# A second layer whose fourth product is also split once more: small sums of A22 by seeds and adding DMAs, a new order of 81 steps

## The chip, the cores and the metric

The kernel runs on one core of a Trainium2 chip. Its engines run side by side, each with its own queue of instructions that it takes strictly in order: TensorE (PE, matmuls; PEld is its weight loads), VectorE (DVE), ScalarE (ACT), GpSimd (POOL) and SyncE (SP, which issues most DMAs). They wait for one another on semaphores. Sixteen DMA engines move data for all queues. The metric is device time in microseconds (us).

## The reference, cut to what matters

```python
w = softmax(weight, axis=-1)                          # 8 heads x 7 taps
x_unf = x_pad[:, idx, :].reshape(B, S, K, H, group)   # B 8, S 4096, D 192
x = np.einsum('hk,bskhg->bshg', w, x_unf).reshape(B * S, D)
h = x @ w_in                                          # 32768 x 192 @ 192 x 2048
g = h * np.clip(h + 3.0, 0.0, 6.0) / 6.0
return (g @ w_out).astype(np.float32)                 # @ 2048 x 192
```

A causal convolution of seven taps along the tokens, one weight per head and tap, then a two-layer network with a hard swish between the layers. Everything is in 32-bit floats.

## The kernel before, in words

Tokens go in 32 blocks of 1024, two groups of 512. Block 0 is special (weights are rounded and loaded beside it, its second layer is direct); blocks 1 to 31 run the same loop: first layer, second layer.

**First layer** (`first_layer`, L443). Sixteen units of 18 matmuls; w_in and the convolved tokens y are split into high and low parts so that three fast passes make a product. A unit fills two banks of PSUM (one of four slots), ACT makes the clipped term from it (`relu`, L306), DVE multiplies (`gate`, L310), and g is in SBUF. Units 0 to 7 make A11 and A22 (token half and half of the 2048 hidden features), units 8 to 15 make A21 and A12; each Aij has eight chunks of 128 features by 512 tokens. Units 0 to 7 read `y_own`, units 8 to 15 read `y_other`, the same data with the upper and lower 64 partitions exchanged by DMA (`swap_parts`). Behind the units stand jobs: taps of the next block's convolution (L806, DVE, behind units 1, 5 and 9), the small sums of A11 (`small_sums`, L491, POOL), the differences S3 = A11 - A21 by pairs of chunks (`g_sums`, L380, POOL, the last pair on DVE), and S1 = A21 + A22 written over A21, for the first two pairs by a DMA from POOL that adds to what is there (L470), for the others by DVE (L400).

**Second layer** (`second_layer`, L502). Strassen's scheme with seven products P1 to P7 in place of eight: for example P4 = A22 x T4, P7 = S3 x T3, P2 = A12 x B21, P5 = S1 x T1. Each has 96 output columns, three strips of 32. PE is used as four strips (rows 0 to 31, 32 to 63 and so on of a PSUM bank) that work side by side. Strips 0 to 2 take plain products, one strip of columns each; strip 3 takes P1 and P5. Their first two strips of columns are done by Strassen *once more* (`level_two`, L591): even and odd chunks, the two strips of columns and the two halves of 512 tokens make a 2 by 2 scheme of seven small products, each four matmuls of 256 columns, on four small sums of the token side (128x1024 each) and four of the weights (`w_s`). Their third strip of columns is plain, eight chunks (for P1 five on strip 3 and one each on strips 0 to 2, bank e). Partial results are carried by ACT copies from a bank's rows to others (L608 to L614), where the next product adds on.

The order is written out by hand. `put(j, cost, fn)` gives a matmul to strip j and moves that strip's clock: cost 2 for 512 columns, 1 for 256. `do(t, fn)` places a job of another engine at time t of the same clock. All are sorted by clock and issued in that order (L686), so t says where an instruction stands in its engine's queue, and nothing waits for a clock: an engine starts the next instruction of its queue as soon as its semaphores allow. A second layer is 82 steps for each strip:

```python
        for q in range(NQ):
            plain(q, d, 4, q, every, True)
            before = (1, 6, NP)[q]
            plain(q, c, 7, q, every[:before], True)
            plain(q, e, 1, 2, range(5 + q, 6 + q))
...
            plain(q, a, 2, q, every[:6], True)
            plain(q, b, 6, q, every)
            plain(q, a, 2, q, every[6:])
```

Strip q does P4 (16 steps), P7 (16, reads S3), one chunk of P1's third strip of columns (2), P2 (12 and 4), P6 (16, reads S2 = S1 - A11) and P3 (16, reads a second S3 = A12 - S2). Banks are d, e, b, x_, a, c, two each from the PSUM slots of units 12, 13 and 14. The jobs: the split of the next y into high (ACT, L415) at 13 and low (DVE, L418) at 15, swaps to `y_other` (SP) at 18, the load of the x after next and its convolution's first taps from 20 on (L87, L804, L806), the four small sums of S1, written into A22 (`s5`), at 16.2, 30.5 and 34.5 (DVE), S2 and S3 (DVE) at 38, the results' adds, transposes and stores from 62.

Of the kernel before, what the change touches and what calls it, by code (L numbers as in the profile page):

```python
# [8 lines left out]
ALU = mybir.AluOpType  # L9
# [22 lines left out]
def kernel(  # L32
# [35 lines left out]
    xs = ctx.enter_context(tc.tile_pool(name="xs", bufs=1))  # L68
    ys = ctx.enter_context(tc.tile_pool(name="ys", bufs=1))
    ot = ctx.enter_context(tc.tile_pool(name="ot", bufs=1))  # L70
    ps = ctx.enter_context(tc.tile_pool(name="ps", bufs=1, space=bass.MemoryType.PSUM))
# [48 lines left out]
    w_in_parts = [cst.tile([P, NP, K3, P], F32, name=f"w_in{n}") for n in range(3)]  # L120
    y_own = [cst.tile([P, K3, N], F32, name=f"y{n}") for n in range(2)]
    y_other = cst.tile([P, 2, K3, N], F32, name="y_other")
    w_out = cst.tile([P, NP, 7, DH], F32, name="w_out")
    B11, B12, B21, B22, T1, T2, T4 = range(7)
    T3 = B12
    w_s = cst.tile([P, 2, 4, NP // 2, QS], F32, name="w_s")

    w_in_bits = moe_w_in.bitcast(U32).rearrange("(p s) (c f w) -> c p s f w", s=K3, f=P, w=2)
# [259 lines left out]
    def rows(q):  # L388
        return slice(q * QS, (q + 1) * QS)
# [51 lines left out]


    def first_layer(i, jobs):  # L443

        def unit(n):
            slot = free_slots.pop(0)
            for m_ in range(3):
                for s in range(K3):
                    products(n, slot, s, (m_,), s == 0, s == K3 - 1)
            to, both = places(n, slot)  # L450
            relu(to, both)
            gate(to, both)
            free_slots.append(slot)

        count = 2 * NP
        for job in jobs.get(-1, ()):
            job()
        for n in range(count):
            unit(n)
            for job in jobs.get(n, ()):  # L460
                job()
            if n == 1:
                s1.append(ot.tile([P, NP, N], F32, name="s1", tag="shared")[:])
            if n < NP and n % 2:
                small_sums(s1[-1], A11, (1, 2, 3, 4), nc.gpsimd, every[n - 1 : n + 1])
            if n > NP and n % 2:
                pair = slice(n - NP - 1, n - NP + 1)
                g_sums(nc.gpsimd if n + 1 < count else nc.vector, (3,), range(NP)[pair], 2)
                if n + 3 < count:
                    nc.gpsimd.dma_start(out=S1[:, pair], in_=A22[:, pair], accum_op=ALU.add)  # L470
        for pair in (slice(NP - 2, NP), slice(NP - 4, NP - 2)):
            add(S1[:, pair], A21[:, pair], A22[:, pair])

    TH = N // 2
# [17 lines left out]

    def small_weights(to, w):

        b11, b12, b21, b22 = (
            w_out[:, c::2, w, q * QS : (q + 1) * QS] for c in range(2) for q in range(2)
        )
        t1, t2, t3, t4 = (to[:, n] for n in range(4))
        for o, p, q in ((t1, b12, b11), (t2, b22, t1), (t3, b22, b12), (t4, b21, t2)):
            nc.gpsimd.tensor_tensor(out=o, in0=p, in1=q, op=ALU.subtract)  # L500

    def second_layer(i, between):  # L502
        last = i + 1 == NB
        ours = [free_slots.pop(0) for _ in range(3)]
        d, e, b, x_, a, c = (psum[:, 2 * n + k] for n in ours for k in range(2))
        ends = [psum[:, 2 * free_slots[0] + k] for k in range(2)] if last else [b, b]
# [34 lines left out]

        def small(n, m_, out, start=False):

            x, w = prod[n]
            sums, ws = (s1[-1], w_s[:, 0]) if n == 1 else (s5, w_s[:, 1])
            x11, x12, x21, x22 = four_parts(x)
            z1, z2, z3, z4 = four_parts(sums)
            b11, b12, b21, b22 = (
                w_out[:, h::2, w, q * QS : (q + 1) * QS] for h in range(2) for q in range(2)
            )  # L550
            t1, t2, t3, t4 = (ws[:, k] for k in range(4))
            xm, wm = {
# [3 lines left out]
            for u in range(NP // 2):  # L556
                put(3, 1, lambda u=u: matmul(
                    3, out[:, lo], wm[:, u], xm[:, u], start and u == 0
                ))
# [9 lines left out]
        def tiles():  # L569
# [3 lines left out]
            late.update(zip(("p7", "p5", "u3"), (results[0][m, n] for n in range(3))))  # L573

        for q in range(NQ):
            plain(q, d, 4, q, every, True)
            before = (1, 6, NP)[q]
            plain(q, c, 7, q, every[:before], True)
            plain(q, e, 1, 2, range(5 + q, 6 + q))
            do(clock[q], copy, out=e[rows(q + 1)] if q < 2 else p1[third], in_=e[rows(q)])  # L580
            plain(q, c, 7, q, every[before:])
            plain(q, a, 2, q, every[:6], True)
            plain(q, b, 6, q, every)
            plain(q, a, 2, q, every[6:])
            if last:
                plain_by_halves(q, 3, q, 0)
                plain_by_halves(q, 3, q, 1)
            else:
                plain(q, b, 3, q, every)

        def level_two(n, p, chunks, order):  # L591
# [25 lines left out]
            for step in order.split():  # L617
                if step[0] == "x":
                    fill(int(step[1]))
                elif step[0] in "lh":  # L620
                    fill_half("lh".index(step[0]), int(step[1]))
# [4 lines left out]

        level_two(1, lambda: p1, range(5), "1 x5 6 5 2 7 3 4")
        do(14, copy, out=e[first], in_=V)
        level_two(
# [4 lines left out]
        for t, job in between:  # L634
            do(t, job)
        for t, n in ((16.2, 1), (16.2, 2), (30.5, 3), (34.5, 4)):
            do(t, small_sums, s5, S1, (n,), nc.vector)
        do(32, tiles)
        do(34, lambda: copy(out=late["p7"], in_=c[m]))
        do(38, copy, out=b[m], in_=p1[:])  # L640
        do(38, g_sums, nc.vector, (2,), every, 4)
        do(38, g_sums, nc.vector, (4,), every, 4)
        do(62, lambda: add(late["u3"], b[m], late["p7"]))
        do(62, lambda: add(late["p7"], late["u3"], d[m]))
        do(62, lambda: store(i, late["p7"], 1, 0))
        do(66, add, p1[:], a[m], p1[:])
        do(66, lambda: store(i, p1, 0, 0))

# [33 lines left out]
        if last:  # L682
            do(74, end_lower)
        else:
            do(82, lambda: copy(out=late["p5"][third], in_=V))
        events = sorted(((t, fn) for st in streams for t, fn in st), key=lambda x: x[0])  # L686
# [28 lines left out]
    with tc.manual_schedule():  # L715
# [142 lines left out]

        def split_high():
            high_of(y_own[HIGH][:], y[:])  # L860

# [11 lines left out]
        def begin_block_two():  # L873
            w_sums(((T1, B12, B11), (T2, B22, T1), (T4, B21, T2)))
            for n, w in enumerate((B11, T1)):
                small_weights(w_s[:, n], w)
            conv.extend(conv_jobs(2))
            for job in conv[:3]:
# [16 lines left out]
        S3 = last.tile([P, NP, N], F32, name="s3")[:]  # L895
        p1 = last.tile([DH, N], F32, name="p1")
        left = []
        for i in range(1, NB):
# [10 lines left out]
            if i + 1 < NB:  # L909
                between = [(13, split_high), (15, split_rest), (18, swap_parts)]  # L910
            if i + 2 < NB:
# [35 lines left out]
```

## Time and profile before

| what | value |
|---|---|
| median of 3 runs | 2220.81 us (2220.73 to 2221.07) |
| profiled execution: time, span from first to last instruction | 2220.6 us, 2218.5 us |
| granted TensorE clock | 1.000 |
| PE, DVE, ACT, POOL busy | 2211.4, 1808.9, 935.8, 827.9 us |
| DMAs from SP and others, share of 16 engines (queue q1) | 105.86 MB, 23.7% |
| DMAs from POOL (queue q0) | 33.64 MB, 8.8% |
| one adding DMA (L470), 512 KB, issue to landing | 5.0 us median |

The chain of waits is the view to start with: it goes back from the last instruction to whatever released each one, and its shares say which engine set the end (PE 99%). A timeline lists one engine's instructions in order with their start and length, and in brackets the idle time ahead of one and who ended it. Windows give busy time per engine in stretches of time, then the granted clock, the share of the DMA engines, and GB/s. Matmuls in 32-bit floats appear as two passes each.

### The profile page before, as it was taken

The numbers are of one execution on the slowest core, as the hardware profiler recorded it, in microseconds if no ns is written. First come the engines' busy times: TensorE is split into PE (matmuls) and PEld (weight loads), VectorE is DVE, ScalarE is ACT, GpSimd is POOL, SyncE is SP. The second block draws the span as 40 slices with busy tenths as digits, with TensorE's granted clock in tenths as the row PEclk, the third lists the DMA queues.
The fourth block names the chain that finished last, engine by engine and source line by source line (L and its number), as shares of the span: only waits on it lengthen the run. The fifth ranks groups of instructions, "written<-read, shape, count | busy, mean of one in ns | idle before, by whom it ended". The sixth has DMA issues, their size and how long they took to land.

```text
span 2218.5 us, 49343 instructions
## 1 busy us (share of the span) xinstructions
PE 2211.4 (100%) x21598; PEld 1535.2 (69%) x21598; DVE 1808.9 (82%) x1588; ACT 935.8 (42%) x1172; POOL 827.9 (37%) x706
## 2 busy tenths in 40 slices
PE   9999999999999999999999999999999999999999
PEld 5567776677776677766777667776667776677766
DVE  8878788888888888888888888888888888888866
ACT  7434443344433444433444334443344433344433
POOL 4434442244422344323444224442244432344322
PEclk9999999999999999999999999999999999999999
DMA  7333323433223332243332333322433224333232
GB/s 165 65 71 69 66 37 67 77 63 77 35 58 78 70 70 49 44 77 70 70 62 40 68 74 66 77 35 59 77 68 73 43 49 77 70 70 57 40 59 34
DMA packets 249095, 142.91 MB, mean 64 GB/s; under 512 B 207120, under 2 KB 212240, under 8 KB 248880
## 3 DMA queue, kind: packets, MB, share of 16 engines
q1 hardware_dynamic: 230392, 105.86, 23.7%
q0 software_dynamic: 17248, 33.64, 8.8%
q8 instruction: 169, 2.77, 0.5%
q10 hardware_dynamic: 1240, 0.27, 0.1%
q14 instruction: 46, 0.38, 0.1%
HBM read 31.72 MB, written 25.17 MB: 26 GB/s over the span
## 4 chain that ended last, share of the span: by engine, by line
PE 99%; ACT 0%; DVE 0%; POOL 0%; DMA 0%; issue 0%; POOLq 0%; ACTq 0%; DVEq 0%
PE psum L528 50%; PE psum L432 47%; PE psum L321 2%; PE psum L730 0%; PE psum L738 0%; ACT g L306 0%; DMA y_other<-y 0%; POOL w_in L220 0%; ACT scale L196 0%; ACT sig L193 0%; ACT sig L199 0%; POOL sig L210 0%; ACT w_in L218 0%; DVE y L283 0%; POOLq L942 0%
## 5 line engine op out<-in xcount | busy, mean ns | idle before, releaser
L528 PE MATMUL psum<-g,w_out 128*32 128x512 f32 (+1 forms) x6712 | 967.4, 552 | 0.0
L306 ACT ACTIVATE g<-psum,half 128x1024 f32<-128x1024 f32 x512 | 572.3, 1118 | 494.0 <-PE psum L432 465.8
L310 DVE SCALAR_TENSOR_TENSOR g<-g,psum 128x1024 f32<-128x1024 f32 x512 | 618.8, 1218 | 195.1 <-ACT g L306 194.8
L491 POOL TENSOR_TENSOR s<-g 128x256 f32<-128x256 f32 x248 | 268.8, 1084 | 1252.5 <-DVE g L310 915.9
L528 PEld LDWEIGHTS psum<-g,w_out 128*32 128x32 f32 x6712 | 370.8, 110 | 246.9 <-issue 126.7
L432 PE MATMUL psum<-y,w_in 64*128 64x512 f32 x4608 | 534.8, 388 | 0.3
L432 PE MATMUL psum<-y_other,w_in 64*128 64x512 f32 x4608 | 529.0, 386 | 0.1
L432 PEld LDWEIGHTS psum<-y,w_in 64*128 64x128 f32 x4608 | 428.6, 184 | 121.3 <-issue 26.0
L432 PEld LDWEIGHTS psum<-y_other,w_in 64*128 64x128 f32 x4608 | 431.6, 184 | 91.1 <-DMA y_other<-y 0.5
L528 PE MATMUL psum<-s,w_out 128*32 128x512 f32 (+1 forms) x3272 | 465.4, 570 | 0.0
L806 DVE SCALAR_TENSOR_TENSOR y<-x,c_sb,y 128x1536 f32<-128x1536 f32 x186 | 334.8, 1800 | 2.1 <-ACT y L804 1.0
L380 POOL TENSOR_TENSOR s<-g 128x1024 f32<-128x1024 f32 x93 | 297.8, 3202 | 25.1 <-DVE g L310 25.1
L528 PE MATMUL psum<-g,w_s 128*32 128x256 f32 x1240 | 282.8, 379 | 0.0
L528 PEld LDWEIGHTS psum<-s,w_out 128*32 128x32 f32 x3272 | 153.7, 110 | 80.1 <-issue 48.3
L528 PEld LDWEIGHTS psum<-g,w_s 128*32 128x32 f32 x1240 | 136.4, 110 | 68.3
L380 DVE TENSOR_TENSOR s<-g 128x2048 f32<-128x2048 f32 (+1 forms) x93 | 177.1, 1931 | 1.1
L528 PE MATMUL psum<-s,w_s 128*32 128x256 f32 x744 | 170.7, 379 | 0.0
L491 DVE TENSOR_TENSOR g<-g 128x1024 f32<-128x1024 f32 x124 | 151.7, 1224 | 5.3
L380 DVE TENSOR_TENSOR g<-g 128x2048 f32<-128x2048 f32 x62 | 139.0, 2283 | 0.0
L400 DVE TENSOR_TENSOR p<-psum,p 32x256 f32<-32x256 f32 (+1 forms) x93 | 47.7, 513 | 96.5 <-PE psum L528 95.1
L400 DVE TENSOR_TENSOR results<-psum,results 32x256 f32<-32x256 f32 (+3 forms) x128 | 69.3, 541 | 50.8 <-issue 47.3
L525 ACT COPY psum<-psum 32x512 f32<-32x512 f32 x93 | 51.3, 551 | 135.4 <-PE psum L528 135.4
(88 smaller groups left out, 1089.1 us busy)
## 6 DMA issues: line engine op xcount, KB each, us to landing
y_other<-y SPq DMA_DIRECT2D x124, 384.0 KB, 4.9
g<-g POOLq DMA_DIRECT2D x62, 512.0 KB, 5.0
out_dram<-results SPq DMA_DIRECT2D x378, 64.0 KB, 2.0
x<-in_x_dram SPq DMA_DIRECT2D x53, 388.5 KB, 7.1
g<-in_moe_w_in_dram SPq DMA_DIRECT2D x16, 192.0 KB, 5.7
stage<-in_moe_w_out_dram SPq DMA_DIRECT2D x8, 384.0 KB, 5.7
x<-in_x_dram SPq DMA_DIRECT2D x7, 384.0 KB, 6.5
y_other<-y SPq DMA_DIRECT2D x12, 128.0 KB, 2.3
```

Source lines behind the costliest of these rows:

```text
L306: nc.scalar.activation(r6, h, ACT.Relu, bias=half[:], scale=1.0 / 6.0)
L310: nc.vector.scalar_tensor_tensor(out=g_, in0=g_, scalar=1.0, in1=h, op0=ALU.min, op1=ALU.mult)
L321: lambda p=p: nc.tensor.matmul(out=bank[j * QS : (j + 1) * QS, tokens], lhsT=w_out[:, p, w, cols], rhs=x[:, p, tokens], start=(first and p ...
L380: engine.tensor_tensor(out=o[:, r], in0=a[:, r], in1=b[:, r], op=op)
L400: nc.vector.tensor_tensor(out=out, in0=x, in1=y, op=op)
L432: nc.tensor.matmul(out=psum[:, 2 * slot + k], lhsT=r32(w_in_parts[wn][r, c, s]), rhs=r32(y_other[r, yn, s] if group else y_own[yn][r, s]), ...
L491: engine.tensor_tensor(out=o, in0=p, in1=q, op=op)
L525: streams[3].append((t - 0.5, lambda: fn(*args, **kw)))
L528: nc.tensor.matmul(out=out, lhsT=w, rhs=x, start=start, stop=True, tile_position=(0, j * QS), skip_group_check=True,)
L806: jobs.append(lambda k=k: nc.vector.scalar_tensor_tensor(out=y[:], in0=x[:, :, k : k + N], scalar=c_sb[:, k : k + 1], in1=y[:], op0=ALU.mu ...
```

## The change

P4's first two strips of columns are now done by the same small scheme, on A22. Its seven small products stand on strips 0, 1 and 2 (1, 2 and 5; 6 and 3; 7 and 4), beside P1's and P5's on strip 3. With it:

- Four small sums of A22 are made. ACT writes "seeds" (copies with a sign, `seed`) into new tiles `z` and `z_early` behind units 7, 9 and 10; POOL issues DMAs that add to them (`onto`): onto all of z behind unit 8 (1 MB, in pieces of 256 floats), S1's first four chunks behind unit 11 in one DMA (1 MB, before two of 512 KB), z's second half onto the first `z_early` tile (512 KB) right behind it, ahead of unit 13's S3 difference, and that tile onto the second `z_early` tile (512 KB) at the end of the layer. Two sums have the other sign, and `w_s4` (made once, with a negated B22 from ACT) takes it up.
- `z_early` shares its memory with `y_own` (a pool `yo`, tags y0 and y1). So the split of the next y moves from 13 and 15 to 33.5 and 42, the swaps from 18 to 45. The x load stays at 20.
- The order of strips 0 to 2 is written out anew up to step 45: P4's plain chunks for the third strip of columns are shared by the three strips (bank b, copied on from strip to strip), S3 is read from step 0 on strips 1 and 2, and its later chunks from step 14 on strip 2. P6 begins at 45, not 50. Strip 3 gives half a chunk of P1 to strip 2 and starts with plain chunks.
- P4 is gathered in a new SBUF tile `p4`, not read from bank d; two more DVE adds of 32x256 belong to it. The small sums of S1 keep one in z, since x22 of A22 is read until step 65. Due times move (below).

```diff
+        s4_sums = {
+            NP - 1: [lambda: seed(z[:, :, 0], x11, -1.0), lambda: seed(z[:, :, 1], x21, 1.0)],
+            NP: [lambda: onto(z[:].rearrange("p u c t -> p (u c) t"), A22[:, :, halves[1]])],
+            NP + 1: [begin_sums],
+            NP + 2: [lambda: seed(sums_a22()[3], x12, -1.0)],
+        }
...
-                if n + 3 < count:
-                    nc.gpsimd.dma_start(out=S1[:, pair], in_=A22[:, pair], accum_op=ALU.add)
+                if n == NP + 3:
+                    onto(S1[:, : NP // 2], A22[:, : NP // 2])
+                    onto(sums_a22()[1], z[:, :, 1])
...
+        onto(sums_a22()[3], sums_a22()[1])
...
-        d, e, b, x_, a, c = (psum[:, 2 * n + k] for n in ours for k in range(2))
+        d, e, b, c, a, x_ = (psum[:, 2 * n + k] for n in ours for k in range(2))
...
+        plain(0, t4, 4, 2, (0,), True)
+        plain_half(0, t4, 4, 2, 2, 0)
+        do(clock[0], copy, out=t4[second], in_=t4[first])
+        small4(0, 1, d[first], True)
+        do(clock[0], copy, out=B4, in_=A4)
+        plain(0, c, 7, 0, every[:2], True)
+        small4(0, 2, d[first])
+        do(clock[0], copy, out=p4[first, lo], in_=A4)
+        plain_e(0)
+        small4(0, 5, d[first, TH:], True)
...
+        plain(1, c, 7, 1, every[:4], True)
+        plain_half(1, t4, 4, 2, 2, 1)
+        plain(1, t4, 4, 2, (1, 4, 6))
+        do(clock[1], copy, out=t4[third], in_=t4[second])
+        plain(1, c, 7, 1, every[4:])
+        plain_e(1)
+        small4(1, 6, d[second])
+        do(clock[1], copy, out=C4, in_=B4)
+        plain(1, a, 2, 1, every[:4], True)
+        small4(1, 3, d[second])
...
+        plain(2, c, 7, 2, every[:4], True)
+        plain(2, a, 2, 2, every[:3], True)
+        plain(2, c, 7, 2, every[4:])
+        plain(2, t4, 4, 2, (3, 5, 7))
...
         for q in range(NQ):
-            plain(q, d, 4, q, every, True)
...
+            assert clock[q] == 45
             plain(q, b, 6, q, every)
...
-        level_two(1, lambda: p1, range(5), "1 x5 6 5 2 7 3 4")
-        do(14, copy, out=e[first], in_=V)
+        level_two(1, lambda: p1, range(4), "x4 half 1 5 6 2 7 3 4")
+        do(9, copy, out=e[first], in_=V)
...
-        for t, n in ((16.2, 1), (16.2, 2), (30.5, 3), (34.5, 4)):
-            do(t, small_sums, s5, S1, (n,), nc.vector)
+        for t, n in ((18, 1), (18, 3), (26.5, 2)):
+            do(t, sum_s5, n)
...
+        do(37, g_sums, nc.vector, (2,), every[:4], 4)
+        do(41.5, add, p4[second, lo], B4, p4[second, lo])
+        do(41.5, g_sums, nc.vector, (2,), every[4:], 4)
+        do(44, sum_s5, 4)
+        do(44, g_sums, nc.vector, (4,), every[:4], 4)
...
-                between = [(13, split_high), (15, split_rest), (18, swap_parts)]
+                between = [(33.5, split_high), (42, split_rest), (45, swap_parts)]
```

## The prediction

> **What bounds the kernel now.** I read four views: busy times, the chain of waits, the waits, and a timeline of one block. TensorE (PE) is busy for 2211.4 of 2218.5 us, and the chain that ended last alternates between the two layers:
>
> ```profile
> PE 2211.4 (100%) x21598; PEld 1535.2 (69%) x21598; DVE 1808.9 (82%) x1588; ACT 935.8 (42%) x1172; POOL 827.9 (37%) x706
> ```
> ```profile
> 1119.74 32.87 PE psum L432 x288
> 1152.62 35.47 PE psum L528 x216
> ...
> 2177.72 35.40 PE psum L528 x279
> ```
>
> Columns of the second: start, length, what. The reader is to see no gap: a block is 32.87 us of first layer and 35.47 us of second, and in the list of waits PE waits for nobody. So the gain is whatever leaves PE's program, and the loss is whatever makes PE wait for the first time. A second layer of `before` is 82 steps on each of four strips (from the code), so a step is 35.47/82 = 0.4326 us.
>
> **What goes.** In the built programs the steps of L528 fall from (4184 x 2 + 1800)/4 = 2542 to 2511 per strip: one per block, 31 in all. Term A: 31 x 0.4326 = **-13.4 us**. Every block also gets 32 more 256-column matmuls and 18 fewer of 512. Do short ones cost extra? In `before` the last block has all four strips on 256 columns near its end:
>
> ```profile
> 2210.31 0.39 PE L528 MATMUL psum<-s,w_out 128*32 128x256 f32 x3
> 2210.47 0.38 PE L528 MATMUL psum<-g,w_out 128*32 128x256 f32 x1
> 2210.53 0.39 PE L528 MATMUL psum<-s,w_out 128*32 128x256 f32 x3
> ```
>
> Each pass starts 0.22 us after the last on its strip, two passes a step, and that block takes 35.40 us for 82 steps. I cost short matmuls at nothing. New are strips that start a 512-column matmul at odd steps; the bounds are 0 and half a step where the phase changes (0.22 x some 4), and I take 0, nearest to this row.
>
> **What is added, by engine (one block, times of the block above; the second layer's step n is at 1152.6 + 0.4326n).**
>
> *ACT*: four seeds of 128x1024 (L477). No such row; L415 copies 128x1536 in 1.48 us, L306 128x1024 out of PSUM in 1.12; so 1.0 to 1.12, I take 1.05. Two stand behind relu 7 (ends 1137.5), one behind relu 9, one behind relu 10. ACT sits idle 0.92 us before each relu, so relu 8 starts 1.2 us late, relu 11 about 0.9, and relu 12 or 13 is on time. A unit's PSUM is wanted again three units (6.2 us) after its end, and relu and gate take 2.4: hidden. If the cover were gone, every 0.1 us late would cost 3 us. ACT's twelve more copies of 0.34 to 0.58 us fall into gaps of 0.4 to 4 us; their readers come five steps (2.16 us) later, and today's four-step gaps make no PE wait.
>
> *DVE*: two adds of 0.43 us more. The split of y (1.75) and one sum (1.22) move behind step 37, where only 1.5 us are idle. DVE then ends some 2 us behind PE, not 0.4 ahead; since it today waits 1.1 us for a copy there, the next block's first gate slips 1.3 us, to 1127.2 in these times, and PE wants that PSUM at unit 4, 1128.0. Hidden with 0.7 us to spare. Earlier due times (S2 at step 45, S3 at 65) keep 1.1 us or more.
>
> *POOL and the DMA engines*: here the cover is thin.
>
> ```profile
> 1141.36 0.73 POOL L491 TENSOR_TENSOR s<-g,s 128x256 f32<-128x256 f32 x1
> 1142.87 3.91 POOL L380 TENSOR_TENSOR s<-g 128x1024 f32<-128x1024 f32 x1 [0.78 <-DVE g L310]
> 1147.08 1.21 POOL L470 DMA_DIRECT2D g<-g  x1 [0.30 <-POOL s L380]
> 1147.83 2.92 POOL L380 TENSOR_TENSOR s<-g 128x1024 f32<-128x1024 f32 x1
> 1151.04 1.20 POOL L470 DMA_DIRECT2D g<-g  x1 [0.30 <-POOL s L380]
> 1151.79 2.86 POOL L380 TENSOR_TENSOR s<-g 128x1024 f32<-128x1024 f32 x1
> ```
> ```profile
> 1148.00:1152.20 4.20, 4.20 (x40) 3.48 (x38) 2.57 (x3) 2.23 (x2) 3.90 (x4) 1.00 0.72 125
> 1157.00:1170.00 13.00, 13.00 (x154) 7.81 (x147) 9.78 (x10) 4.69 (x10) 0.00 (x0) 1.00 0.82 183
> ```
>
> The last two numbers of a window are the DMA engines' share and GB/s. The first window holds one adding DMA of 512 KB: 4.2 x 0.72 = 3.0 us of all sixteen engines; traffic begins 1.8 us after issue, and it lands 5.0 us after issue (list of DMA issues). The second holds 2313 KB of swaps and x loads: 10.7 us, 4.6 us per MB, so an x load (777 KB) is 3.6 us.
>
> The change makes 1 MB of adds into 3 MB, in a chain: z (1 MB, behind POOL's small sums, 1142.1, so traffic from 1143.9), S1 (1 MB, after gate 11, traffic from about 1152.3), z2 (0.5 MB, needs z), z4 (0.5 MB, needs z2). By bytes that is 6.0 + 6.0 + 3.0 + 3.0 us. z and z2 go in pieces of 1 KB where the old row has 2 KB. Bounds: the same per byte (6.0) and the same per piece, 12.0. The 128-byte stores (2.65 us of engines for 3072 pieces, 14 ns each, in their own window) lie near the rate per byte; I take 6.3 and 3.15.
>
> A transfer that moves: the built program now puts SP's x load ahead of the swaps. In `before` it issued at 1161.56, behind them; now it waits only for the conv tap behind gate 9 (about 1145) and runs beside z. That holds in 22 blocks; in 7 more a memset on DVE holds it until about 1162. Engine time in a row from 1143.9: z 6.3 + x 3.6 + S1 6.0 + z2 3.15 = 19.05, so z2 lands at 1163.0 + 0.4 = 1163.4. Step 25 (strip 1, sixth small product) is at 1163.4. Then z4: issue 1163.5, landing 5.0 later, 1168.5; step 37 is at 1168.6. With DVE's lag of about 0.3 us I take **0.2 us** of waiting in 22 blocks, and 0.3 in the 7 where x runs beside z4: Term B = 4.4 + 2.1 = **+6.5 us**. Lower bound 0, when x fills gaps that the adds leave; upper bound, if pieces set the price, over 5 us a block.
>
> POOL's order adds a risk: z2's issue stands ahead of the last S3 sum on POOL and waits for z. z lands between 1151 and 1154.6; the issue is 1.2 us, the sum 2.3 to 2.9, and DVE's two-input sums hold POOL up (3.91 against 2.9 above, while a tap runs). S3 is there at 1155 to 1158.7; steps 14 and 15 (strips 2 and 1) read it at 1158.7. Taken as 0.
>
> The set-up's four w_s4 sums fall into POOL's 14.6 idle us before block 1: nothing.
>
> The Trainium skill, "DMA: Bandwidth & Descriptors", Anatomy of one DMA, fits a DMA from POOL as 2.0 us plus bytes at 436 GB/s. That is an estimate of 3.2 us for 512 KB, where this trace has 5.0 from issue to landing. By the page the chain would be microseconds early, Term B zero and the time 2207.2; the measurement decides.
>
> **Sum.** Profiled execution 2220.6 (span 2218.5 and 2.1 around it; the median shown is 2220.81): 2220.6 - 13.4 + 6.5 = 2213.7, called **2213**. The bound for telling a change from none is 0.2%, 4.4 us.
>
> **Rivals.**
> 1. *The DMA chain is the new bound.* For it: the margins above are 0 to 0.1 us, and adds and loads share sixteen engines that would be full for 19 us. It decides above 0.46 us of wait per block (13.4/29). At 1.0 us in 29 blocks: 2220.6 - 13.4 + 29 = **2236**; at 2 us, 2265. The Trainium skill, same page, Issuing engines are not separate DMA queues, says that DMAs of all issuers run on the same engines and interleave; the additive 10.7 us above agree.
> 2. *POOL's last S3 sum is late*, its DMA issue being dearer for 1024 pieces than for 256 or z late: about 0.8 us in 22 blocks, 2220.6 - 13.4 + 17.6 = **2225**. Against it: the margin is 0 to 3 us.
> 3. *Nothing is late*: 2220.6 - 13.4 = **2207**.
> 4. *PE does not keep 0.4326 us per step* with strips out of phase: half a step per block lost at two places gives back the whole gain, **2221**. Against it: strips already run free of each other, 0.16 us apart.
>
> **Chances.** Forecast (waits of a few tenths, 2208 to 2216): 0.31. Rival 1: 0.29. Rival 2: 0.13. Rival 3: 0.16. Rival 4: 0.11. Faster by over 0.2%: 0.45 (forecast and rival 3 nearly whole); within: 0.15 (rival 4 and edges of 1 and 2); slower: 0.40. The range runs from rival 3 to a wait of about 1.2 us a block, 2207 to 2243, and leaves out the far end of rival 1. The forecast's own range is 2208 to 2216.
>
> **What would show it.** A second layer of 35.04 us in the chain is Term A alone; each tenth above is wait. PE waiting for a DMA into z0 at step 25 or z1 at step 37 is Term B or rival 1; for POOL's s3 at step 14, rival 2; longer spacing of passes without a wait, rival 4. An x load not issued near 1145 of such a block breaks Term B; gates later than unit 4's start break the cover named for DVE.

## The result, and the profile after

The changed kernel takes **2370.69 us** (2370.15 to 2371.19, four runs) where the kernel before takes 2220.84: a ratio of 1.0675, 95% interval 1.0656 to 1.0693. It is 150 us slower, far outside the range on record. The granted clock is 0.999.

First the busy row of the page, then one block of the chain of waits (start, length, what):

```profile
PE 2316.5 (98%) x22466; PEld 1506.4 (64%) x22466; DVE 1904.6 (80%) x1650; ACT 1156.3 (49%) x1545; POOL 891.2 (38%) x772
```
```profile
1119.66 33.33 PE psum L437 x288
1152.99 4.86 PE psum L568 x29
...
1157.93 0.56 ACT psum L565
...
1158.54 10.59 PE psum L568 x74
...
1170.29 0.59 ACT y L420
...
1171.69 0.38 ACT p L715
...
1172.11 1.08 PE psum L568 x11
...
1173.29 0.43 DVE p L405
...
1173.76 19.06 PE psum L568 x126
```

The chain of before ran from PE to PE. Here it leaves PE three times in each second layer, for ACT or DVE. The second layer is 1192.82 - 1152.99 = 39.83 us, and 81 steps of 0.4326 would be 35.04: 4.79 us are lost. The first layer is 33.33 instead of 32.87, 0.46 more. If every block lost this, 31 x (4.79 + 0.46) = 163 us, less the 13.4 of the saved step, would be the 150.

No DMA is in this block's chain. The list of waits says what the strips' weight loads waited for (total us, times, longest):

```profile
PEld psum L568 <- ACT psum L565: 58.4, 62, 1.2
PEld psum L568 <- ACT p L715: 47.0, 31, 1.6
PEld psum L568 <- DVE p L405: 33.1, 31, 1.1
...
PEld psum L568 <- DVE results L405: 21.0, 31, 0.7
```

31 times is once a block, 62 twice. The sum is 159.5 us; PE as a whole is idle for only 44 of them (rows of PE: 19.0, 17.3 and 8.0), since matmuls whose weights are already loaded still run. All four strips share one queue: an instruction of one strip that waits holds up those of the others behind it. In the 1.54 us before 1172.11 no strip loads a weight, and then eight loads begin within 0.1 us. The chain of adding DMAs, issued by POOL, ran like this:

```profile
1142.27 1.55 POOL L480 DMA_DIRECT2D z<-g  x1
...
1150.04 1.30 POOL L480 DMA_DIRECT2D g<-g  x1 [0.30 <-POOL s L385]
1154.12 1.31 POOL L480 DMA_DIRECT2D z<-z  x1 [2.78 <-DMA z<-g]
...
1163.32 0.90 POOL L480 DMA_DIRECT2D z<-z  x1 [5.50 <-ACT p L712]
```

z is issued at 1142.27 (predicted 1142.1) and lands 11.3 us later, at 1153.6; z2 lands at 1162.75, 8.63 us after its issue, and z4 is issued 0.57 us later, at 1163.32 (predicted 1163.5; the ACT copy that the last line names ended in between). z4 lands at 1168.44. Steps 25 and 37, had they come on time, would have been at 1163.81 and 1169.00: the margins were thin, as expected, but PE does not wait for z, and its readers were themselves late.

**Theory (banks).** In the built programs the framework guards PSUM by whole banks (2 KB of a partition, 512 columns): before a matmul that writes rows 0 to 31 of a bank it puts a wait for ACT's or DVE's last read or write of *any* rows of that bank ahead of it in the program. In the changed kernel such waits stand at steps 9, 37, 39 and 61, each for a copy or sum that is due at that very step (a "zero gap"), and ACT does not start such a copy at once. In the block shown, weight loads wait there for 1.17, 1.54, 1.07 and 0.68 us. A gap of one step, at step 4, makes them wait 0.71: it is the other wait a block of the first row above. At step 37 strip 1 writes bank d for B4, while C, a term of the third strip's scheme, lies in rows 96 to 127 of the same bank and is being copied out:

```profile
1169.70 0.59 ACT L749 COPY results<-psum 96x512 f32<-96x512 f32 x1
1170.18 1.48 ACT L420 ACTIVATE y<-y 128x1536 fp32r<-128x1536 f32 x1
1171.69 0.37 ACT L715 COPY p<-psum 32x256 f32<-32x256 f32 x1
```

This is ACT's timeline. The copy of C (L715, 0.37 us) is third, behind P7's copy and the split of y, and PE goes on at 1172.11, when it ends. No data passes between the two. In the kernel before, P4 left bank d at step 16, and by the order of its code the shortest such gap was two steps. **Rivals:** the chain of adding DMAs (rival 1 of the prediction), or the extra copies and seeds as such.

### The profile page after: what moved, and what is told of

Read it like the earlier page. It is cut to its first block, busy times and chain, and to the rows that moved or that the text cites. A ratio compares the mean times of both kernels' runs of the same rounds, so it can differ in the third digit from the quotient of the medians.

```text
span 2369.1 us, 51730 instructions
## 1 busy us (share of the span) xinstructions
PE 2316.5 (98%) x22466; PEld 1506.4 (64%) x22466; DVE 1904.6 (80%) x1650; ACT 1156.3 (49%) x1545; POOL 891.2 (38%) x772
## 4 chain that ended last, share of the span: by engine, by line
PE 93%; ACT 3%; issue 2%; DVE 1%; DMA 0%; ACTq 0%; POOL 0%; DVEq 0%; SPq 0%
PE psum L568 46%; PE psum L437 45%; PE psum L326 2%; ACT y L420 1%; ACT psum L565 1%; ACT results L749 1%; DVE p L405 1%; ACT p L715 0%; PE psum L844 0%; DMA z<-z 0%; PE psum L852 0%; ACTq L749 0%; DMA out_dram<-results 0%; DMA y_other<-y 0%; DVE results L405 0%
## 5 line engine op out<-in xcount | busy, mean ns | idle before, releaser
L568 PE MATMUL psum<-g,w_out 128*32 128x512 f32 (+1 forms) x6092 | 1048.4, 532 | 8.0 <-ACT psum L565 8.0
L568 PE MATMUL psum<-s,w_out 128*32 128x256 f32 (+1 forms) x3272 | 682.5, 571 | 0.0
L568 PEld LDWEIGHTS psum<-g,w_out 128*32 128x32 f32 x6092 | 364.5, 109 | 266.4 <-issue 91.2
L568 PE MATMUL psum<-g,w_s 128*32 128x256 f32 x1488 | 342.1, 379 | 0.0
L568 PEld LDWEIGHTS psum<-s,w_out 128*32 128x32 f32 x3272 | 221.4, 109 | 106.8 <-issue 74.3
L568 PE MATMUL psum<-z,w_s 128*32 128x256 f32 x992 | 214.3, 381 | 36.4 <-ACT p L715 19.0
L385 DVE TENSOR_TENSOR s<-g 128x2048 f32<-128x2048 f32 (+1 forms) x93 | 229.2, 2465 | 1.1
L568 PEld LDWEIGHTS psum<-g,w_s 128*32 128x32 f32 x1488 | 161.0, 110 | 92.6 <-DVE results L405 21.0
L528 DVE TENSOR_TENSOR g<-g 128x1024 f32<-128x1024 f32 x93 | 111.2, 1223 | 85.9 <-PE psum L568 83.6
L568 PE MATMUL psum<-s,w_s 128*32 128x256 f32 x744 | 170.7, 379 | 0.0
L565 ACT COPY psum<-psum 32x512 f32<-32x512 f32 (+1 forms) x217 | 106.3, 490 | 127.6 <-PE psum L568 126.1
L480 POOL DMA_DIRECT2D z<-z x62 | 67.5, 1089 | 268.5 <-ACT psum L565 64.1
L568 PEld LDWEIGHTS psum<-z,w_s 128*32 128x32 f32 x992 | 89.4, 109 | 102.3 <-ACT p L715 47.0
## 6 DMA issues: line engine op xcount, KB each, us to landing
z<-g POOLq DMA_DIRECT2D x31, 1024.0 KB, 11.4
```

The lines of the kernel that those rows point to most:

```text
L385: engine.tensor_tensor(out=o[:, r], in0=a[:, r], in1=b[:, r], op=op)
L480: nc.gpsimd.dma_start(out=to, in_=x, accum_op=ALU.add)
L528: engine.tensor_tensor(out=o, in0=p, in1=q, op=op)
L565: streams[3].append((t - 0.5, lambda: fn(*args, **kw)))
L568: nc.tensor.matmul(out=out, lhsT=w, rhs=x, start=start, stop=True, tile_position=(0, j * QS), skip_group_check=True,)
```

## Experiments: bank or DMA

"Second layer" is from the chain of waits; the line numbers shift by a few from kernel to kernel (L568 is L569 or L572 in some).

**no_z_dmas**, the changed kernel without its three adding DMAs on z:

```diff
-            NP: [lambda: onto(z[:].rearrange("p u c t -> p (u c) t"), A22[:, :, halves[1]])],
-                    onto(sums_a22()[1], z[:, :, 1])
-        onto(sums_a22()[3], sums_a22()[1])
```

> The changed kernel without its three adding DMAs on z; A22's small sums stay bare seeds, so the first two column strips of P4's result are not the reference's. Everything else, the seeds and the order of the steps too, is kept. DMA-chain theory (the time goes to z, S1, z2 and z4 landing late on one POOL queue): the second layer falls from 39.83 to about 35.0 us and the run from 2370.7 to 2210 to 2225. Bank theory (P4's new products sit in PSUM banks in which ACT and DVE still read other rows, so that PE strips wait for copies, not for DMAs): 2355 to 2372, the second layer 39.4 to 39.9 us, and PE's waits for the copies of lines 565 and 715 stay in the list of waits.

Measured: 2370.53 us (one run). Taking away 2 of the 3 MB changes 0.2 us. With the banks as they are, the loss is not the DMAs'.

**c_apart**, C in a PSUM slot of its own:

```diff
-        B, C, V = (bank[rows(3)] for bank in (x_, d, b))
+        B, C, V = (bank[rows(3)] for bank in (x_, psum[:, 2 * free_slots[0] + 1], b))
-        do(clock[2], add, p4[second, hi], C4, p4[second, lo])
+        do(41.5, add, p4[second, hi], C4, p4[second, lo])
```

> The changed kernel with the third product's term C (a partial sum of 32 rows) in a PSUM slot of its own instead of rows 96 to 127 of bank d, where P4's products of steps 36 to 39 and P5's of 61 start; the addition that reads C goes from 39 to 41.5. Bank theory: the losses at steps 33 to 41 (2.35 us a block) and 53 to 65 (0.73 us) go, a new one of up to 0.8 us may come at step 41 where the copies of line 715 stand behind two others on ACT: the second layer 36.7 to 37.6 us, the run 2275 to 2305. DMA-chain theory: these steps wait for z1 and z4 to land, whatever bank they write: no change, 2365 to 2375.

Measured: 2291.20 us, 79 less, from another address and the place of one DVE add. Chain of waits of c_apart:

```profile
1115.93 4.86 PE psum L568 x29
...
1120.87 0.56 ACT psum L565
...
1121.48 31.61 PE psum L568 x225
```

The two later breaks are gone; the first, at step 9, is still there. The second layer is 1153.09 - 1115.93 = 37.16 us.

**banks_apart**: c_apart, with B in the slot's other bank, t4 out of V's bank, two of the six banks exchanged, and split_high behind the copies:

```diff
-        d, e, b, c, a, x_ = (psum[:, 2 * n + k] for n in ours for k in range(2))
+        d, x_, b, c, a, e = (psum[:, 2 * n + k] for n in ours for k in range(2))
+        other = [psum[:, 2 * free_slots[0] + k] for k in range(2)]
+        B, C, V = (bank[rows(3)] for bank in (x_ if last else other[0], other[1], b))
-        t4 = b
+        t4 = x_
-                between = [(33.5, split_high), (42, split_rest), (45, swap_parts)]
+                between = [(38.5, split_high), (42, split_rest), (45, swap_parts)]
```

> The changed kernel with all bank conflicts that were found taken apart: C and B in PSUM slots of their own, t4 in another bank than V, the six banks of the second layer in another order, split_high at 38.5 and the addition that reads C at 41.5. The DMAs, seeds and the number of steps stay. Bank theory: the second layer 35.0 to 35.4 us instead of 39.83, the first layer still 33.34, the run 2220 to 2232. DMA-chain theory: 2360 to 2375, or as much of the loss as the DMAs make.

Measured: 2265.69 us, ratio to the kernel before 1.0202 (1.0185 to 1.0219): more than expected. The second layer is 36.32 us, with one break left, after 4.45 us (0.56 us of ACT). I had overlooked a zero gap: the copy of V, due at 9, writes bank e, and term A of strip 3, also in e, begins at 9.

**banks_apart2**: A and E change places.

```diff
-        A, E = e[rows(3)], a[rows(3)]
+        A, E = a[rows(3)], e[rows(3)]
```

> banks_apart with one more edit: the third strip's terms A and E change places, so that the strip that starts A at step 9 no longer writes the bank into which ACT copies the 32 rows of V at step 9. Bank theory (the one zero gap left in banks_apart is what still cost it 36.32 instead of 35.04 us a second layer): the chain's break after 4.45 us of the second layer goes, 35.0 to 35.2 us, the run 2226 to 2232. Rival (what is left comes from seeds or DMAs sharing ACT and POOL, not from a bank): 2262 to 2268, the break stays.

Measured: 2282.21 us (ratio 1.0277, 1.0262 to 1.0292), *slower* by 16.5 than banks_apart. A miss, and an instructive one. The break at step 9 is gone, as expected, and a longer one has come at step 41, where strip 0 writes bank a and the copy of A is due. ACT's timeline there:

```profile
1054.97 0.58 ACT L566 COPY psum<-p 96x512 f32<-96x512 f32 x1
1055.50 1.48 ACT L420 ACTIVATE y<-y 128x1536 fp32r<-128x1536 f32 x1
1057.00 0.34 ACT L709 COPY psum<-psum 32x256 f32<-32x256 f32 x1
```

PE waits for the last row, a copy of 0.34 us behind a split of 1.48 us that I had put there myself. The price of this zero gap was set by what was queued ahead on the reader's engine. Its list of waits also names DMAs into z (PEld: 9.4 us, 14 times), which come up again below.

**banks_apart3**: banks_apart with the order of strip 3 changed, so that no zero gap of this kind is left.

```diff
-        level_two(1, lambda: p1, range(4), "x4 half 1 5 6 2 7 3 4")
-        do(9, copy, out=e[first], in_=V)
+        level_two(1, lambda: p1, range(4), "x2 1 x2 half 5 6 2 7 3 4")
+        do(13, copy, out=e[first], in_=V)
+        plain(0, c, 7, 0, every[2:3])
         plain_e(0)
         small4(0, 5, d[first, TH:], True)
-        plain(0, c, 7, 0, every[2:])
+        plain(0, c, 7, 0, every[3:])
```

> banks_apart with no step left at which a strip writes a bank that ACT or DVE still reads for a copy due at that step: the third strip's order becomes two chunks of V, term A, the other chunks of V (x2 1 x2 half), the copy of V goes from 9 to 13, and strip 0 starts its part of that bank at 17 instead of 15. A and E stay where banks_apart has them. Bank theory: the break after 4.45 us of the second layer goes and no other comes, the second layer 35.0 to 35.3 instead of 36.32 us, the run 2225 to 2235. Rival (the rest of the loss is a cost of the seeds, copies or DMAs that no bank explains): 2255 to 2270.

Measured: 2245.31 us (ratio 1.0112, 1.0097 to 1.0127), between the two ranges expected. In its chain PE no longer waits for ACT or DVE before the last block, but block periods vary from 68.4 to 71.0 us, and the list of waits now names DMAs into z (PEld: 12.4 us, 16 times). That is another cause, taken up below.

**c_in_a**, the reverse: the kernel *before*, with C in bank a and E in d. No instruction is added, removed or moved.

```diff
-        B, C, V = (bank[rows(3)] for bank in (x_, d, b))
-        A, E = e[rows(3)], a[rows(3)]
+        B, C, V = (bank[rows(3)] for bank in (x_, a, b))
+        A, E = e[rows(3)], d[rows(3)]
```

> The kernel before with two words changed: term C in rows 96 to 127 of bank a instead of bank d, and E in d instead of a, so that no instruction is added, removed or moved, but strips 0 to 2 write bank a at steps 34, 38 and 62 just behind a DVE or ACT read of C that is due at those steps. Bank theory: three zero gaps at 0.7 to 1.3 us a block each (banks_apart paid 1.28 for one, its ACT being free), 2286 to 2342, with PE and PEld waits for lines 400 and 614. Rival (waits cost only where ACT is crowded by the change's own copies, or the loss is not the banks): 2219 to 2225.

Measured: 2288.24 us (one run), 67.4 more than before, 2.18 us a block. Its list of waits (L611 to L614 are ACT's copies, L400 is DVE's sums):

```profile
PEld psum L528 <- DVE results L400: 32.8, 31, 1.1
PEld psum L528 <- ACT p L614: 29.1, 31, 0.9
...
PEld psum L528 <- DVE p L400: 19.0, 31, 0.6
```

Three rows, 31 times each, where the kernel before has none of the three. By the code and by their times in the block, two are zero gaps, at steps 38 (ACT) and 62 (DVE). The third (`p`, 0.6 us) is not the one expected at step 34: it comes at step 68, two steps behind a DVE sum of bank a that is due at 66. So a gap of two steps can cost too, when the reader's engine is late. Bank sharing alone, without a single new copy, seed or DMA, makes such a loss. The Trainium skill, "PSUM — Partial Sum Buffer", section "PSUM bank collisions raise a hardware error", gives the rule: "Semaphore-guard PSUM by **bank × quadrant** (by bank is the simple version), not by address." A quadrant is 32 partitions. The guard in this kernel is the simple version. No run here takes the finer guard, so what it would save is open.

## Experiments: the slower first layer

The loss of 0.46 us per first layer is all in units 0 to 7, which read `y_own`: their matmuls take 393 ns instead of 388 after the change. The change gave these tiles a pool of their own, so they lie elsewhere in SBUF.

**y_moved** is the kernel before with that alone:

```diff
+    yo = ctx.enter_context(tc.tile_pool(name="yo", bufs=1))
-    y_own = [cst.tile([P, K3, N], F32, name=f"y{n}") for n in range(2)]
+    y_own = [yo.tile([P, K3, N], F32, name=f"y{n}") for n in range(2)]
```

> The kernel before with one edit alone: the two own y tiles are allocated from the pool of their own that the changed kernel gives them, so that they lie elsewhere in SBUF (169408 and 175552 instead of 118944 and 125088 bytes into a partition; multiples of 64 bytes instead of 32 bytes past one). Theory that the place makes the first layer's reads slower: units 0 to 7 (those that read these tiles) go from 2.04 to 2.10 us, a block's first layer from 32.87 to about 33.34, the run from 2220.8 to 2234 to 2237. Rival (the slower units come from the change's DMAs, seeds or order): 2219 to 2222, units 0 to 7 at 2.04 us.

Three variants of y_moved shift the tiles by a pad that nothing uses: **y_pad** (32 bytes ahead of them), **y_pad_front** (32 bytes at the front of the constants), **y_pad224** (224 bytes ahead of them).

```diff
+    yo.tile([P, 8], F32, name="pad")      # y_pad
+    cst.tile([P, 8], F32, name="pad")     # y_pad_front
+    yo.tile([P, 56], F32, name="pad")     # y_pad224
```

> y_moved with a tile of 32 bytes per partition, used by nothing, ahead of the own y tiles in their pool: these then start 32 bytes past a multiple of 64 (169440 and 175584), as in the kernel before, in the place of y_moved. Address theory (a first-layer read from a tile at a multiple of 64 bytes is slower): units 0 to 7 back at 2.04 us, the run 2219 to 2223. Rival (the region or the order of the pools makes it slower, not the 32 bytes): 2234 to 2238 as y_moved.

> y_moved with the 32-byte tile at the front of the constants instead, so that the own y tiles start 32 bytes past a multiple of 64 and y_other, the first layer's weights and g start at one. Address theory, if only the y tile counts: units 0 to 7 at 2.04 us and units 8 to 15 (which read y_other) at 2.10, the run 2234 to 2238. If it is the place of y against that of the weights (both at the same remainder is fast): both groups slow, 2248 to 2253. If the region counts: units 0 to 7 slow alone, 2234 to 2238.

> y_moved with 224 bytes instead of 32 ahead of the own y tiles: y0 then lies a multiple of 512 bytes from the first-layer weights w_in0 (87552 bytes), as in the kernel before (36864) and as y_other does; it was 288 past one in y_moved and in y_pad_front, 320 in y_pad. Theory that this distance sets the pace of units 0 to 7: 388 ns a matmul again instead of 393, the run 2219 to 2222. Rival (the region, or being a multiple of 64 or 32 alone): 2226 as y_pad, or 2234 to 2236 as y_moved.

| kernel | y0 past 64 bytes | y0 minus w_in0, past 512 bytes | ns a matmul, units 0 to 7 | time, ratio to before |
|---|---|---|---|---|
| before | 32 | 0 | 388 | 2220.8 |
| y_moved | 0 | 288 | 393 | 2235.97, 1.0068 (1.0053 to 1.0083) |
| y_pad | 32 | 320 | 390 | 2226.64, 1.0027 (1.0016 to 1.0037) |
| y_pad_front | 32 | 288 | 393 | 2236.03 (one run) |
| y_pad224 | 32 | 0 | 388 | 2220.80, 1.0000 (0.9991 to 1.0010) |

y_moved is where it was expected: the place costs 15.2 us, a tenth of the whole loss. My first reading, a multiple of 64 bytes, fell with y_pad_front (393 ns at 32 past one), and with y_pad, which came back only in part. The distance to the first-layer weights, taken modulo 512 bytes, sorts all five, and the changed kernel with them (288, 393 ns); y_pad224 was predicted by it and hit. The groups of instructions of y_moved and of y_pad224:

```profile
L433 PE MATMUL psum<-y,w_in 64*128 64x512 f32 x4608 | 548.5, 393 | 0.2
```
```profile
L434 PE MATMUL psum<-y,w_in 64*128 64x512 f32 x4608 | 534.8, 388 | 0.3
```

Count and shape are the same, and so are the clocks; only the mean differs. Whether it is the distance to the weights or to other tiles of that pool (they all lie at multiples of 512 from one another) is not told apart, nor by what mechanism.

**apart2_pad** is banks_apart2 with y_pad's tile:

> banks_apart2 with the 32-byte tile of y_pad: the change with its bank conflicts and its y tiles' place mended, the DMAs, seeds and 81 steps kept. Both theories together: first layer 32.87, second layer 35.0 to 35.2 us, the run 2209 to 2217, below the kernel before by 4 to 12. If Term A is not real (a step saved is lost elsewhere): 2219 to 2223.

Measured: 2278.55 us (ratio 1.0264, 1.0249 to 1.0279), a miss. It shares banks_apart2's new gap, so its number says little; its units 0 to 7 take 390 ns, as in y_pad.

## Experiments: what the banks had hidden

**apart3_cst**: banks_apart3 with y and z_early taken from the constants' pool, at the addresses of before.

```diff
-        return [yo.tile([P, K3, N], F32, name=f"{name}{n}", tag=f"y{n}") for n in range(2)]
+        return [cst.tile([P, K3, N], F32, name=f"{name}{n}", tag=f"y{n}") for n in range(2)]
```

> banks_apart3 with the own y tiles and the z tiles that follow them taken from the constants' pool, one tag each, so that they start where y0 and y1 do in the kernel before (118944 and 125088). Seeds, adding DMAs, small sums of A22 and the 81 steps are kept. Bank and place theories together: first layer 32.87, second layer 35.0 to 35.3 us, the run 2207 to 2217, which is below the kernel before. If the saved step does not pay by itself: 2219 to 2223.

Measured: 2242.18 us (ratio 1.0097, 1.0080 to 1.0113), 25 above the range. The first layer is back at 32.87 us, and the best blocks take 67.9 us, as Term A wants, but others up to 70.2. Waits of its weight loads:

```profile
PEld psum L569 <- DMA z<-z: 15.7, 17, 1.9
PEld psum L569 <- POOL s L385: 12.3, 19, 1.6
```

These are the prediction's rivals 1 and 2, 17 and 19 times in 31 blocks: z4 not landed at step 37 (all 17 waits come 15.9 to 18.2 us into the second layer; z2 is never waited for at step 25), and POOL's last S3 sum queued behind z2's issue (steps 14 and 15).

**apart3_no_z** takes the three adding DMAs out of apart3_cst (the three lines of no_z_dmas); **early_z** keeps them and issues z ahead of POOL's last small sums:

```diff
-            NP - 1: [lambda: seed(z[:, :, 0], x11, -1.0), lambda: seed(z[:, :, 1], x21, 1.0)],
-            NP: [lambda: onto(z[:].rearrange("p u c t -> p (u c) t"), A22[:, :, halves[1]])],
+            NP - 1: [lambda: seed(z[:, :, 0], x11, -1.0), lambda: seed(z[:, :, 1], x21, 1.0),
+                     lambda: onto(z[:].rearrange("p u c t -> p (u c) t"), A22[:, :, halves[1]])],
```

> apart3_cst without its three adding DMAs on z; A22's small sums stay bare seeds, so the first two column strips of P4's result are not the reference's. Seeds, copies, banks, y's place and the order of the steps are kept. Chain theory (z, z2 and z4 land late, and POOL's last S3 sum queues behind z2's issue, now that no bank wait hides it): PE's waits for z and for POOL's line 385 go, the second layer 35.03 us in every block, the run 2206 to 2214. Rival (seeds and copies cost the rest): 2235 to 2244.

> apart3_cst with the first adding DMA issued one place earlier on POOL's queue, ahead of the last four small sums of S1's unit pair instead of behind them. Chain theory: z is issued about 3 us earlier (it waits for its seeds on ACT, not for POOL), z2 and the last S3 sum follow 2 to 3 us earlier, and most of the waits for z and for line 385 go: 2207 to 2220, below the kernel before. S1's last small sums come 1.5 us later, which has cover until step 13. Rival (lateness is of the DMAs' own pace, or the loss is not theirs): 2235 to 2244.

Measured: apart3_no_z 2211.53 us (ratio 0.9959, 0.9943 to 0.9974), all 30 block periods 67.90 or 67.91; early_z 2221.83 (1.0005, 0.9996 to 1.0015), 1.8 above its range. The same removal that was worth 0.2 us in the changed kernel is worth 30.7 here: the DMAs' lateness had been hidden behind the banks'. Seeds and copies, all still in place, cost nothing that a block period shows.

**z2_first** puts z2's DMA ahead of S1's on POOL's queue; **z2_first_s5** also moves two DVE sums from step 18 to 25.

```diff
-                    onto(S1[:, : NP // 2], A22[:, : NP // 2])
                     onto(sums_a22()[1], z[:, :, 1])
+                    onto(S1[:, : NP // 2], A22[:, : NP // 2])
-        for t, n in ((18, 1), (18, 3), (26.5, 2)):
+        for t, n in ((25, 1), (25, 3), (26.5, 2)):     # z2_first_s5 only
```

> early_z with z2's adding DMA issued ahead of S1's on POOL's queue instead of behind it. If S1's transfer holds z2 up: z2 lands 6 to 7.5 us after its issue instead of 11.4, z4 is issued 3 to 4 us earlier, no wait of PE for z is left, 2211 to 2217, below the kernel before; S1 lands some 2 us later and DVE waits for it in a gap. If the three transfers share one rate whatever their order: 2219 to 2224.

> z2_first with DVE's two sums that read S1 moved from step 18 to 25, behind which nothing waits before step 49. If DVE's wait for the later S1 costs anything in z2_first, this run is 1 to 4 us faster than it; if not, the same within 1.5 us: 2210 to 2217. If the transfers share one rate: 2219 to 2224.

Measured: 2229.30 us (ratio 1.0038, 1.0024 to 1.0052) and 2228.95 (1.0036, 1.0022 to 1.0050); both miss. z2 now takes 5.7 us from issue to landing in the median of 31 (10.9 in early_z), z4 8.4 (4.9), and since z4 is issued earlier no wait for z is left. But S1 lands 11.4 us after its issue instead of 8.2, DVE waits for it (90.5 us in all in z2_first), and PE waits for DVE's sums behind that. Order on one queue only moved the lateness.

**split_z**: early_z, with z's DMA cut in two. The half that z2 reads goes first, z2 ahead of S1, the other half (read at step 35) last.

```diff
-            NP - 1: [lambda: seed(z[:, :, 0], x11, -1.0), lambda: seed(z[:, :, 1], x21, 1.0),
-                     lambda: onto(z[:].rearrange("p u c t -> p (u c) t"), A22[:, :, halves[1]])],
+            NP - 1: [lambda: seed(z[:, :, 1], x21, 1.0), lambda: onto(z[:, :, 1], x22),
+                     lambda: seed(z[:, :, 0], x11, -1.0)],
...
+                if n == NP + 1:
+                    onto(sums_a22()[1], z[:, :, 1])
                 if n == NP + 3:
                     onto(S1[:, : NP // 2], A22[:, : NP // 2])
-                    onto(sums_a22()[1], z[:, :, 1])
+                if n == NP + 5:
+                    onto(z[:, :, 0], x21)
```

> early_z with z's 1 MB adding DMA cut in two: the half that z2 reads goes first, behind one seed instead of two, z2 follows behind POOL's first S3 sum and ahead of S1, and the other half of z, read at step 35, behind POOL's third S3 sum. If transfers queue behind each other in POOL's order and each is paid by its bytes: z2 lands some 4 us earlier than in early_z and S1 no later than 1.5 us, no wait for z and none for S1 is left, the second layer 35.04 us in nearly every block, 2211 to 2216, below the kernel before. If the sum of the bytes in this stretch decides: 2218 to 2226.

Measured: 2218.67 us (ratio 0.9990, 0.9981 to 0.9999): above its range, and inside that of the rival (the bytes decide). But PE waits for no DMA; about every second block takes 67.9 us, and the others 68.1 to 68.6. DVE's timeline in one of these:

```profile
1161.30 2.36 DVE L531 TENSOR_TENSOR g<-g 128x1024 f32<-128x1024 f32 x2 [2.32 <-DMA z<-g]
1163.69 0.96 DVE L405 TENSOR_TENSOR p<-psum,p 32x256 f32<-32x256 f32 x2
```

A sum of S5 overwrites the part of A22 that z's second half is read from. It waits 2.32 us for that transfer, and the partial sums of PSUM (L405), which PE wants, stand behind it on DVE.

**split_z_s3** moves that sum behind them; its reader comes at step 57.

```diff
-        for t, n in ((18, 1), (18, 3), (26.5, 2)):
+        for t, n in ((18, 1), (26.5, 2), (33.5, 3)):
```

> split_z with one edit: DVE's sum that overwrites the part of A22 read by z's second half goes from step 18 to 33.5, behind the partial sum of step 33; its reader comes at step 57. If that wait is what every second block still pays: 67.91 to 68.0 us in all blocks, 2211 to 2214 (apart3_no_z, which has no adding DMA on z, took 2211.5), below the kernel before by 7 to 10. If the transfers collide with something else in those blocks (x, the output): 2216 to 2220.

Measured: **2211.37 us**, ratio 0.9956 (0.9943 to 0.9970): faster than the kernel before by 9.4 us, the whole computation kept. All 30 block periods are 67.90 or 67.91 us. Its chain of waits runs from PE to PE again:

```profile
1113.34 32.86 PE psum L437 x288
1146.21 35.04 PE psum L572 x257
1181.25 32.86 PE psum L437 x288
```

## Why the prediction was wrong, point by point

**Where the 163 us above 2207.4 (2220.8 less Term A) went**, by the runs in their order: banks 125.4 (2370.7 to 2245.3, banks_apart3); y's place 3.1 in that order (to 2242.2), because, it seems, late DMAs take up most of what it gives back (weight loads wait 15.7 us for z and 12.3 for POOL in apart3_cst, 12.4 and 2.8 in banks_apart3), and 15.2 alone (y_moved); the adding DMAs 30.8 (to 2211.4, split_z_s3); 4.0 left over, which lie in the last block (77.7 us from the start of its first layer to the end of the span, against 73.7 before). The prediction costed that block like any other. Its chain leaves PE 27.2 us into the second layer and runs mostly on DVE from there, where before PE held it for 35.40; among DVE's instructions there is an S3 sum of 2.29 us. No run tests this.

- **The step that failed** is the one on ACT: its twelve more copies "fall into gaps of 0.4 to 4 us; their readers come five steps (2.16 us) later, and today's four-step gaps make no PE wait". That holds for the readers of the copied data, and I looked at nothing else. It fails for the *writers of the same bank*, which come at the same step and wait until the copy is through. The question "which instruction may not start until this one is done with the bank?" was not asked. The code had it: in the changed kernel `d` is P4's bank in steps 3 to 64, and `C` is `d[rows(3)]`. Measured, with its DVE counterpart: 125 us. No rival named it, which is why the range missed too. The list of waits of before even has a row of this kind, against "PE waits for nobody":

```profile
PEld psum L528 <- ACT psum L525: 13.8, 62, 0.2
```

One of its two waits a block comes at step 22: by the code, strip 3 writes rows 96 to 127 of bank e two steps behind a copy from rows 0 to 31 to rows 32 to 63. It cost PE nothing there, but gaps of four steps were not the shortest.

- **Term A** was right in blocks 1 to 30: 35.47 to 35.04 us a second layer (split_z_s3), 0.43 each. So was nothing for 256-column matmuls, for starts at odd steps (rival 4 falls) and for seeds: 1.05 us each, hidden in apart3_no_z.
- **Term B** was mis-sized, and at first invisible. Predicted 6.5 us for z4 and nothing for the S3 sum; with the banks mended the adding DMAs cost 30.7 (apart3_cst against apart3_no_z), 1.0 us a block. In the list of waits 15.7 us are z4's and 12.3 the S3 sum's, so it is rivals 1 and 2 together. z4's transfer was sized well: 4.8 us in the median of 31, where the sum had 5.0, and up to 6.2. What failed is its margin of 0.1 us. z2 lands 11.0 us after the second layer's start, where the sum had 10.8; z4 is issued 0.6 behind that, not 0.1, and lands at 16.5 in the median, behind step 37 (16.0). Transfers that overlap on POOL's queue cost each other: z2 takes 11.4 us behind S1's 1 MB in a block of early_z, and S1 11.4 instead of 8.2 behind z2 in z2_first.
- The x load did move to 1144.96 in the block above, beside z, and in all 29 blocks that load one, not in 22. DVE's lag has its cover: the first layer is 32.86 us in split_z_s3.
- **Rival 2** was taken as 0 and exists (12.3 us of POOL waits in apart3_cst), by one of the two causes it named: z is late. It lands 2.0 us after the second layer's start in the median there, at the late end of the -1.6 to 2.0 that was forecast, and up to 3.5; z2's issue takes 1.3 us, near the 1.2 assumed.
- **The place of y**, moved by the pool `yo`, was costed at nothing without a word. It is 15.2 us, more than Term A.
- The Trainium skill, "DMA: Bandwidth & Descriptors", Anatomy of one DMA, has a fit that estimates 3.2 us for 512 KB. It is not borne out here: in the changed kernel z2 takes 8.5 us and z4 4.6 in the median.

## What to carry to other kernels

When an instruction is put beside others in PSUM, list for each bank who reads or writes it from ACT or DVE and which matmul writes it next, whatever rows they use. With the guard of this kernel a gap of zero steps there stops all strips until the reader is through, with what stands ahead of it in its queue (1.3 us a block for the one left in banks_apart, 2.2 for the three waits of c_in_a, one of them at a gap of two steps). Mend the loudest wait and measure again before judging the others: the DMA chain was worth 0.2 us in the changed kernel and 30.7 once the banks were apart. A sound saving (13.4 us) was buried three times over, and each layer had its own signature in the list of waits.

## What the runs showed of the hardware that was not expected

The pace of a matmul changed with the place of its moving operand: 388, 390 and 393 ns at 0, 320 and 288 bytes past a multiple of 512 from the stationary operand's tile, the same instructions at the same clock, 15 us in 2221. Three distances were tried; whether this distance or another one is what counts is open. Tiles of the second layer in other places (s against g, 592 and 593 ns in the kernel before) show no such difference.
